# Three quarters of w_out issued behind a transpose's landing, and the second batch's k, q and v loaded a period later

## The chip, the cores and the metric

The kernel runs on one core of a Trainium2 chip. The metric is the device time of one execution in microseconds (us). The engines are PE (matrix products and transposes), DVE and ACT (element-wise work), POOL (element-wise work, and it issues DMAs) and SP (it issues DMAs). A DMA is issued from an engine's queue, in that queue's order, and lands some microseconds later.

## The reference

Thresholded attention for 8 batches of 8 heads (576 rows of 64) feeds a two-layer network over 4608 rows.

```
scores = (q @ k^T) / sqrt(64)
keep scores >= max(row) - tau, the others become -1e9        # tau = 0.02
attn = softmax(scores);   x = attn @ v                       # heads side by side: 4608 x 512
h = x @ w_in              # 512 x 2048
g = max(0.01 * h, h)
out = g @ w_out           # 2048 x 512
```

## The kernel before, in words

The work is cut into *periods*, numbered through the whole run by `n`. A period is one block of 128 rows of one batch for two pairs of heads (four heads); a batch has eight such periods, and for each two batches there are two more for the last 64 rows. Periods 0 to 7 are batch 0, period 8 is the first of batch 1. The loop at L633 issues, in an order written out by hand, the work of several stages that belong to different periods, and each engine runs its part of this list strictly in order.

For period `n` the stages are:

- **Scores** (`scores`, L302; the matmuls are at L297). Two row halves of PE run side by side. At one point the halves use the same bank of PSUM, so the last piece of the first half waits for a *signal*: an empty instruction on another engine that itself waits for the matmul before it. The list `SIGNAL` says which engine gives it in which period: POOL, except in period 2 and from period 9 on, where it is SP. An engine that gives the signal gives it in its own order, behind whatever it has queued.
- **Copies, exponentials, weights** (L338, L367, L378, L372 and L373) on DVE and ACT.
- **The turn** (`turn_w`, L387). The 128 x 2304 weights are transposed by a DMA that SP issues (L389), for every period from period 3 on; the earlier periods are transposed on PE. The turn of period `n` is issued in iteration `n + 1`. I write "turn 4" for the turn of period 4's weights.
- **pv** (`pv`, L418, matmuls at L426). The product with v of period `n` stands in iteration `n + 2` and needs turn `n`.
- **The network.** When the four pairs of a row block are ready, `layer1` (L456, matmuls L466) runs in four units and `layer2` (L473, matmuls L479) in eight; unit `r` of layer 2 reads `w_out16[:, 2r : 2r + 2]`. Each half of an iteration has two units of layer 2 and one of layer 1. The first row block's layer 2 has units 0 and 1 in iteration 4, 2 to 5 in iteration 5, and 6 and 7 in iteration 6.

Within an iteration PE's order is: scores, transposes of q and k, then the first half (layer 2, layer 1, at times a late transpose of q or k, L211, then pv) and the second half (layer 2, layer 1).

The weights w_in and w_out are loaded by POOL in four quarters each (`load_w`, L121), with a cast from fp32 to fp16; a quarter of w_out has the 512 rows that two units of layer 2 read, one pair of units for each quarter. Quarters 0 and 1 of w_out are issued in iteration 1, quarters 2 and 3 in iteration 4.

The inputs q, k and v are loaded by SP in 512 KB tiles, one for four heads. The dictionaries `loads_at`, `small_at`, `split_at_` and `pool_at` say in which iteration a load or a piece of POOL's work is put into the list; loads by SP stand behind that iteration's turn. For batch 1 the tuple `rows` gives the iterations of k (heads 0 to 3), q (heads 0 to 3), k (heads 4 to 7), q (heads 4 to 7), and `v_at` those of the two halves of v and of its last rows. The last tile of q is loaded in four parts (L86) since PE transposes part of it straight from fp32 (`late32`). POOL splits the others in an iteration before they are transposed: scaled (L160), rounded (L167), rest (L171). The second tile of k is split in iteration 6; behind that split POOL has a widening copy (L253) and two small loads (L93), and then the signal of period 7.

Of the kernel before, what the change touches and what calls it, by code (L numbers as in the profile page):

```python
# [33 lines left out]
def kernel(  # L34
# [10 lines left out]
    nc = tc.nc  # L45
# [24 lines left out]
    def load_main(b, s, which):  # L70
        if (b, s, which) in MIXED:
            return [load_part(b, s, which, t=t) for t in range(4)][0]
        t = sb.tile([128, 4, 256], FP32, tag="raw", bufs=4, name="raw")
        raws[b, s, which] = t
        return nc.sync.dma_start(
            out=t[:, :, :], in_=SRC[which][b, ds(4 * s, 4), 0:MAIN, :].rearrange("h (p t) d -> p h (t d)", t=4))
# [12 lines left out]
    def load_tails(b, which, engines=None, small=nc.sync):  # L89
        t = sb.tile([128, 2, 2, 64], FP32, tag="rawt", bufs=4, name="rawt")  # L90
        src = SRC[which][b, :, MAIN:S, :].rearrange("(u sh) p d -> u p sh d", u=2)
        for u, eng in enumerate(engines or (small, small)):
            eng.dma_start(out=t[ds(64 * u, 64), :, :, :].rearrange("p s h d -> p (s h) d"), in_=src[u])  # L93
        tails[b, which] = t

    def load_v(b, s):
        t = sb.tile([128, 4, 256], FP32, tag="vraw", bufs=2, name="vraw")
        vraws[b, s] = t
        return nc.sync.dma_start(
            out=t[:, :, :], in_=v[b, ds(4 * s, 4), 0:MAIN, :].rearrange("h (p t) d -> p h (t d)", t=4))  # L100

    def load_vtails(b, small=nc.sync):
        t = sb.tile([128, NP, 64], FP32, tag="vrawt", bufs=1, name="vrawt")
        src = v[b, :, MAIN:S, :].rearrange("(r h) p d -> h p r d", h=2)
        for h in range(2):
            small.dma_start(out=t[ds(64 * h, 64), :, :], in_=src[h])
        vtails[b] = t

    def cast_v(b, p, copy=None):
        copy = copy or nc.gpsimd.tensor_copy  # L110
        src = vraws[b, p // 2][:, ds(2 * (p % 2), 2), :].rearrange("p h (t d) -> p h t d", d=64)
        dst = v16[b % 2][:, p, :, :].rearrange("p (h t) d -> p h t d", h=2)
        return [copy(out=dst[:, h, ds(h, 4), :], in_=src[:, h, :, :]) for h in range(2)][0]  # L113

    def cast_vtails(b, copy=None):
        copy = copy or nc.gpsimd.tensor_copy
        t = vtails.pop(b)
        for h in range(2):
            copy(out=v16[b % 2][ds(64 * h, 64), :, 4 + h, :], in_=t[ds(64 * h, 64), :, :])

    def load_w(i):  # L121
        if i < 4:
            return nc.gpsimd.dma_start(out=w_in16[:, :, ts(i, 512)],
                                in_=moe_w_in[:, ts(i, 512)].rearrange("(a p) f -> p a f", p=128))
        else:
            j = i - 4
            return nc.gpsimd.dma_start(out=w_out16[:, ds(4 * j, 4), :],
                                in_=moe_w_out[ds(512 * j, 512), :].rearrange("(j p) f -> p j f", p=128))
# [62 lines left out]
    def unit32(b, which, p0, np=1, t0=0, nt=4):  # L191
        return (b, which, p0, np, t0, nt)
# [64 lines left out]
    periods, first_of = [], []  # L257
# [18 lines left out]
        cut = (a // 512 + 1) * 512  # L276
        return [(a, cut - a), (cut, a + 576 - cut)]

    SIGNAL = [nc.gpsimd, nc.gpsimd, nc.sync] + [nc.gpsimd] * 6 + [nc.sync]
    HALVES = ((0, 0), (1, 0), (0, 1))  # L280

    BEHIND = mybir.DependencyInfo(mybir.DependencyClass.Sync, mybir.DependencyReason.DATA)
# [19 lines left out]
    def scores(st, between=None):  # L302
# [12 lines left out]
        while todo[0] or todo[1]:  # L315
# [14 lines left out]
            if (h, x) == (1, b12) and i == 2:  # L330
                signal = SIGNAL[min(st.n, 9)].nop()
                tc.add_manual_dep(signal.ins, last.ins.name, BEHIND, reason="the row halves share a bank")
# [53 lines left out]

    def turn_w(st):  # L387
        st.wt = sb.tile([128, 2, 9, 128], FP16, tag="wT", bufs=4, name="wT")
        nc.sync.dma_start_transpose(  # L389
            out=st.wt[:, :, :, :].rearrange("k c n q -> k (c n) q"),  # L390
            in_=st.w[:, :, :, :].rearrange("q c n d -> q (c n d)"))

# [112 lines left out]
    loads_at, small_at, turns_at, early32, late32, split_at_, pool_at = {}, {}, {}, {}, {}, {}, {}  # L505

    def at(d, n, f):
        d.setdefault(n, []).append(f)
# [80 lines left out]
    for p in range(NP):  # L589
        at(pool_at, 1 + p // 2, lambda p=p: cast_v(0, p))  # L590
    at(pool_at, 1, lambda: cast_vtails(0))
    for i in range(4):
        at(pool_at, 1 if i < 2 else 4, lambda i=i: load_w(4 + i))

    def split_at(n, key):
        at(split_at_, n - 1, key)
        at(turns_at, n, key)
# [6 lines left out]
    for b in range(1, B):  # L604
        E = 18 * (b // 2)
        if b == 1:
            units = [(0, "k", 4), (0, "q", 5), (1, "q", 6), ("t", "k", 6), (2, "k", 7), (3, "k", 8), ("t", "q", 9)]
            late32[5], late32[7], late32[8] = [unit32(1, "k", 1)], [unit32(1, "q", 2)], [unit32(1, "q", 3)]
            rows, t_at, v_at, casts = (0, 2, 4, 5), (3, 7), (6, 7, 8), (8, 8, 9, 10, 9)
        elif b % 2 == 0:  # L610
            units = [(*u, E - 8 + i) for i, u in enumerate(in_turn)] + [("t", "k", E - 5), ("t", "q", E + 9)]
            rows, t_at, v_at = (E - 11, E - 10, E - 7, E - 6), (E - 8, E + 6), (E - 5, E - 1, E - 4)
            casts = E - 1, E, E + 1, E + 2, E
        else:
            units = [(*u, E + i + i // 4) for i, u in enumerate(in_turn)] + [("t", "k", E + 4), ("t", "q", E + 9)]
            rows, t_at, v_at = (E - 3, E - 2, E + 2, E + 3), (E + 1, E + 6), (E + 1, E + 4, E + 2)
            casts = E + 3, E + 3, E + 6, E + 7, E + 5
        for p, w_, n in units:
            split_at(n, (b, p, w_))
        for i, (s, w_) in enumerate(((0, "k"), (0, "q"), (1, "k"), (1, "q"))):  # L620
            at(loads_at, rows[i], lambda b=b, s=s, w_=w_: load_main(b, s, w_))
        for w_, n in zip("kq", t_at):
            at(small_at, n, lambda b=b, w_=w_, small=nc.sync: load_tails(b, w_, small=small))
        for s in range(2):
            at(loads_at, v_at[s], lambda b=b, s=s: load_v(b, s))
        at(small_at, v_at[2], lambda b=b, small=nc.sync: load_vtails(b, small=small))
        for p in range(NP):
            at(pool_at, casts[p], lambda b=b, p=p: cast_v(b, p))
        at(pool_at, casts[4], lambda b=b: cast_vtails(b))
# [3 lines left out]
    while n < N + PV_LAG or l1q or pending or l2q or stores:  # L633
        st = periods[n] if n < N else None
# [55 lines left out]
        for i, f in enumerate(work):  # L690
            mm = f()
# [11 lines left out]
        if here:  # L703
            o = ps.tile([128, 1024], FP16, tag="o", bufs=1, name="wp")
            if n < 3:
                turn_w_here(before, 6, 6, o[:, 0:768])
        elif before and st:
            turn_w(before)
# [91 lines left out]
```

## Time and profile before

| | |
|---|---|
| median of three runs | 482.44 us (482.31 to 482.67) |
| the profiled execution | 484.03 us, of which the span in the profile is 482.3 us |
| PE busy | 463.1 us, 96% of the span |
| DVE, ACT, POOL busy | 433.2, 420.1, 216.2 us |
| chain of waits, by engine | PE 86%, DMA 5%, DVE 4%, ACT 2% |
| DMA queues | 83.67 MB, 173 GB/s on average |
| granted clock of PE | full speed throughout |

Times in the profile count from the start of the span. The *timeline* gives start, duration, engine, line, name and count of merged instructions, and in brackets how long the engine was idle before and what released it. The *waits* view gives total us, number and longest wait for each pair of waiting and releasing lines. The *chain* is the sequence of work and waits that ended last. For a DMA, SP's and POOL's timelines show only the time that the issue took; "DMA to landing" runs from the start of the issue until the data has arrived and is signalled. One profiled execution stands for all durations.

### The profile page before, as it was taken

Reading aid. Unit: us, or ns where it says so; the run is one execution under the profiler, and the core shown is the slowest. Engines: PE = TensorE matmul, PEld = TensorE weight load, DVE = VectorE, ACT = ScalarE, POOL = GpSimd, SP = SyncE. Lnnn points to the kernel's source line nnn. Section 1 sums busy time; section 2 is a strip of 40 time slices with the busy share of each in tenths; the row PEclk is TensorE's granted clock in tenths of the full one; section 3 lists DMA queues with packets and bytes.
Section 4 is the critical chain, followed back from the end, with each engine's and each line's share of the span. In section 5 each row is a group of like instructions: output and inputs, shape, how many; then the busy total and the mean of one; then the engine's idle time right before and its main releaser. Section 6 shows DMA issues by size and latency. Waiting matters only on the chain.

```text
span 482.3 us, 25139 instructions
## 1 busy us (share of the span) xinstructions
PE 463.1 (96%) x10810; PEld 375.7 (78%) x10810; DVE 433.2 (90%) x1309; ACT 420.1 (87%) x783; POOL 216.2 (45%) x355
## 2 busy tenths in 40 slices
PE   6889889999999999999999999999999999999996
PEld 4668667888888888888888888788888778877774
DVE  3999879999999999999999999999999989999940
ACT  4899779999999999999999999899999889988862
POOL 2645547554565464454465474454466563000000
PEclk9999999999999999999999999999999999999999
DMA  9999999798999978899799988889889995655641
GB/s 176 237 217 197 164 206 201 160 196 182 205 171 202 209 161 188 155 173 211 154 190 202 212 174 201 135 183 193 185 183 193 200 165 124 124 122 123 127 91 46
DMA packets 206271, 83.67 MB, mean 173 GB/s; under 512 B 175280, under 2 KB 200880, under 8 KB 206160
## 3 DMA queue, kind: packets, MB, share of 16 engines
q1 hardware_dynamic: 199184, 74.66, 80.1%
q0 software_dynamic: 5568, 6.95, 7.8%
q8 instruction: 84, 1.38, 1.2%
q10 hardware_dynamic: 1408, 0.46, 0.4%
q14 instruction: 27, 0.22, 0.1%
HBM read 36.70 MB, written 9.44 MB: 96 GB/s over the span
## 4 chain that ended last, share of the span: by engine, by line
PE 86%; DMA 5%; DVE 4%; ACT 2%; issue 1%; SPq 1%; DVEq 0%; ACTq 0%
PE hp L466 25%; PE o L479 25%; PE sc L297 21%; PE pv L426 8%; DMA wT<-w 4%; PE tp L410 3%; PE tp L186 3%; DVE s L338 2%; DVE w L378 1%; DMA raw<-in_k_dram 1%; ACT g L469 1%; DVE qT L239 0%; SPq L86 0%; ACT e L367 0%; DVE kT L239 0%
## 5 line engine op out<-in xcount | busy, mean ns | idle before, releaser
L338 DVE TENSOR_SCALAR_CACHE_REDUCE s<-sc 128x576 f32<-128x576 f32 x288 | 205.5, 753 | 17.4 <-PE sc L297 17.4
L466 PEld LDWEIGHTS <-win 128*64 128x64 f16 x4608 | 146.5, 110 | 28.7 <-DVE xt L437 1.1
L378 DVE SCALAR_TENSOR_TENSOR w<-s,th,e 128x576 f16<-128x576 f32 x213 | 163.8, 817 | 0.2
L367 ACT ACTIVATE e<-s,mn 128x576 f16<-128x576 f32 x213 | 157.8, 778 | 0.0
L479 PE MATMUL o<-wout,g 128*64 128x512 f16 x1152 | 148.8, 379 | 0.3 <-DMA wout<-in_moe_w_out_dram 0.3
L466 PE MATMUL hp<-x,win 128*64 128x128 f16 x4096 | 136.3, 219 | 0.6 <-DVE x L445 0.3
L469 ACT ACTIVATE g<-hp 128x512 f16<-128x512 f32 x144 | 86.1, 598 | 43.7 <-PE hp L466 43.7
L297 PE MATMUL sc<-kT,qT 64*128 64x384 f16 (+7 forms) x1920 | 120.7, 284 | 3.5 <-DVE s L338 1.3
L297 PEld LDWEIGHTS <-qT 64*128 64x128 f16 (+1 forms) x1920 | 90.1, 97 | 20.3 <-issue 2.0
L160 POOL TENSOR_SCALAR scaled<-raw 128x512 f32<-128x512 f32 x53 | 32.7, 616 | 144.8 <-DVE w L378 131.8
L479 PEld LDWEIGHTS <-g 128*64 128x64 f16 x1152 | 58.7, 110 | 29.1 <-issue 0.4
L171 POOL TENSOR_TENSOR half<-scaled,half 128x512 f16<-128x512 f32 (+1 forms) x68 | 71.6, 1054 | 5.8
L373 ACT ACTIVATE w<-s,minus_tau 128x576 f16<-128x576 f32 x75 | 58.2, 776 | 2.4
L372 ACT ACTIVATE s<-s,th 128x576 f32<-128x576 f32 x75 | 57.5, 767 | 0.7 <-DVE th L356 0.7
L426 PE MATMUL pv<-wT,v 128*64 128x128 f16 (+1 forms) x1600 | 53.1, 215 | 5.2 <-DMA wT<-w 3.7
L426 PEld LDWEIGHTS <-v 128*64 128x64 f16 x1600 | 45.8, 110 | 6.9 <-issue 3.7
L167 POOL CAST half<-scaled 128x512 f16<-128x512 f32 (+1 forms) x68 | 38.3, 563 | 4.4
L445 DVE TENSOR_TENSOR x<-pv,by 128x256 f16<-128x256 f32 x64 | 27.1, 424 | 8.1 <-PE pv L426 7.0
L416 ACT COPY by<-tp 128x256 f16<-128x256 f16 x72 | 26.8, 372 | 0.0
L186 PEld LDWEIGHTS <-half 64*128 64x128 f16 x968 | 24.2, 95 | 2.5 <-issue 1.0
L113 POOL CAST v<-vraw 128x256 f16<-128x256 f32 x64 | 24.5, 417 | 0.0
L186 PE MATMUL tp<-ident,half 64*128 64x64 f16 x968 | 24.1, 190 | 0.0
(61 smaller groups left out, 332.9 us busy)
## 6 DMA issues: line engine op xcount, KB each, us to landing
vraw<-in_v_dram SPq DMA_DIRECT2D x16, 512.0 KB, 5.4
out_dram<-osb SPq DMA_DIRECT2D x31, 256.0 KB, 3.9
raw<-in_q_dram SPq DMA_DIRECT2D x13, 512.0 KB, 4.9
raw<-in_k_dram SPq DMA_DIRECT2D x13, 512.0 KB, 5.6
win<-in_moe_w_in_dram POOLq DMA_DIRECT2D x4, 512.0 KB, 10.7
wout<-in_moe_w_out_dram POOLq DMA_DIRECT2D x4, 512.0 KB, 12.5
raw<-in_q_dram SPq DMA_DIRECT2D x12, 128.0 KB, 3.8
raw<-in_k_dram SPq DMA_DIRECT2D x10, 128.0 KB, 4.3
```

The lines of the kernel that those rows point to most:

```text
L171: nc.gpsimd.tensor_tensor(out=halves[key][:, 1, 0:n, :, :], in0=scaled.pop(key)[:, 0:n, :, :], in1=halves[key][:, 0, 0:n, :, :], op=AX.sub ...
L186: nc.tensor.transpose(tps[key][r][:, x, t, :], half[rows, x, t, :, :].rearrange("p h d -> p (h d)"), ident[rows, rows])
L297: yield nc.tensor.matmul(out=o, lhsT=lhs, rhs=turned[st.b, "k"][rows, kx, pair, ds(key0, n)], start=(i == 0), stop=(i == 2), skip_group_ch ...
L338: return nc.vector.tensor_scalar(out=st.s[TILES[n]][:, :], in0=sc[:, ds(PLACE[TILES[n]], 576)], scalar1=-1.0 / UNIT, scalar2=None, op0=AX. ...
L367: nc.scalar.activation(out=st.e[t][:, :], in_=st.s[t][:, :], func=AF.Exp, bias=st.mn[:, n : n + 1], scale=-1.0)
L372: nc.scalar.activation(out=z, in_=z, func=AF.Prelu, bias=st.th[:, n : n + 1], scale=-1.0, alpha=1e20)
L373: nc.scalar.activation(out=w_of(st, t), in_=z, func=AF.Exp, bias=minus_tau[:, :], scale=1.0, accum_out=st.sum[:, c, h : h + 1])
L378: st.last = nc.vector.scalar_tensor_tensor(out=w_of(st, t), in0=st.s[t][:, :], scalar=st.th[:, n : n + 1], in1=st.e[t][:, :], op0=AX.is_le ...
L426: nc.tensor.matmul(out=st.pv[ds(64 * h, 64), c, ts(u, n)], lhsT=v16[st.b % 2][:, pair, blk, :], rhs=st.wt[:, c, blk - (blk > 4), ts(u, n)] ...
L466: nc.tensor.matmul(out=hp[ds(64 * c, 64), jj, :], lhsT=w_in16[:, i, ds(128 * (4 * u + jj) + 64 * c, 64)], rhs=g.x[:, i, :], start=(i == 0) ...
L469: nc.scalar.activation(out=g.g[:, ds(4 * u, 4), :], in_=hp[:, :, :], func=AF.Prelu, bias=0.0, scale=1.0, alpha=0.01)
L479: nc.tensor.matmul(out=g.o[ds(64 * c, 64), :], lhsT=g.g[:, j, ds(64 * c, 64)], rhs=w_out16[:, j, :], start=(j == 0), stop=(j == 15), skip_ ...
```

## The change

Four edits:

1. Quarter 0 of w_out stays in iteration 1. Quarters 1, 2 and 3 are issued by POOL at the end of iteration 4, and quarter 1 waits until turn 3 has landed; 2 and 3 follow it in POOL's order.
2. For batch 1, the second tile of k moves from iteration 4 to 5, the second tile of q from 5 to 6, and the halves of v from 6 and 7 to 7 and 8. On SP each stands behind the next turn, then: k behind turn 4, q behind turn 5, v behind turns 6 and 7.
3. The signal between the row halves of period 5 is given by SP instead of POOL.
4. `turn_w` keeps a handle of its instruction so that the wait can be attached.

The instructions on PE, DVE and ACT and their order are the same as before.

```diff
-    SIGNAL = [nc.gpsimd, nc.gpsimd, nc.sync] + [nc.gpsimd] * 6 + [nc.sync]
+    SIGNAL = [nc.gpsimd, nc.gpsimd, nc.sync, nc.gpsimd, nc.gpsimd, nc.sync] + [nc.gpsimd] * 3 + [nc.sync]
...
     def turn_w(st):
         st.wt = sb.tile([128, 2, 9, 128], FP16, tag="wT", bufs=4, name="wT")
-        nc.sync.dma_start_transpose(
+        st.turn = nc.sync.dma_start_transpose(
...
+    def load_w_out(i):
+        mm = load_w(4 + i)
+        if i == 1:
+            tc.add_manual_dep(mm.ins, periods[3].turn.ins.name, BEHIND, reason="DMA would serve w_out beside the turn")
+        return mm
+
     for i in range(4):
-        at(pool_at, 1 if i < 2 else 4, lambda i=i: load_w(4 + i))
+        at(loads_at if i else pool_at, 4 if i else 1, lambda i=i: load_w_out(i))
...
-            rows, t_at, v_at, casts = (0, 2, 4, 5), (3, 7), (6, 7, 8), (8, 8, 9, 10, 9)
+            rows, t_at, v_at, casts = (0, 2, 5, 6), (3, 7), (7, 8, 8), (8, 8, 9, 10, 9)
```

## The prediction

> **What bounds the kernel now.** The page's table of engines has PE busy for 96% of the span and its chain of waits runs through PE for 86%, so what PE waits for is what time there is to win. The windows view finds where PE idles after the start: not here,
>
> ```profile
> 80.00:85.00 5.00, 5.00 (x138) 3.90 (x126) 4.79 (x17) 4.92 (x10) 4.29 (x7) 1.00 0.74 90
> ```
>
> (PE busy 5.00 of 5.00 us), but at 50 to 55 us (3.34) and 60 to 65 us (2.97). The waits of the first 110 us name the cause (total, times, longest), and the chain of that stretch shows two long turns:
>
> ```profile
> PE pv L426 <- DMA wT<-w: 3.7, 2, 2.0
> PE o L479 <- DMA wout<-in_moe_w_out_dram: 0.3, 1, 0.3
> POOL scaled L160 <- DMA raw<-in_k_dram: 4.7, 1, 4.7
> 42.73 10.75 DMA wT<-w
> 53.56 8.93 DMA wT<-w
> ```
>
> PE's timeline (start, us, name, idle before it) places them. Layer 2 reads the second quarter of w_out at 42.37, the third at 45.66 and the fourth at 50.02; pv of periods 4 and 5 stand at 53.61 and 62.53, the scores of period 7 at 56.05, and the turn of q for pair 2 at 59.84:
>
> ```profile
> 42.37 1.03 PE L479 MATMUL o<-wout,g 128*64 128x512 f16 x8
> 45.66 1.05 PE L479 MATMUL o<-wout,g 128*64 128x512 f16 x8
> 50.02 1.05 PE L479 MATMUL o<-wout,g 128*64 128x512 f16 x8 [0.25 <-DMA wout<-in_moe_w_out_dram]
> 53.61 0.75 PE L426 MATMUL pv<-wT,v 128*64 128x128 f16 x20 [1.65 <-DMA wT<-w]
> 56.05 1.64 PE L297 MATMUL sc<-kT,qT 64*128 64x384 f16 x24
> 59.84 0.66 PE L211 MATMUL tp<-ident,raw 128*128 128x128 f32 x4
> 62.53 0.75 PE L426 MATMUL pv<-wT,v 128*64 128x128 f16 x20 [2.03 <-DMA wT<-w]
> ```
>
> From about 80 us on PE is full, so a shift left there reaches the end one for one. At stake: 1.65 + 0.25 + 2.03 = 3.93 us. The timelines of SP and POOL show what is queued:
>
> ```profile
> 34.79 4.00 SPq L389 DMA_TRANSPOSE wT<-w  x1
> 38.90 0.51 SPq L75 DMA_DIRECT2D raw<-in_k_dram  x1
> 42.73 7.16 SPq L389 DMA_TRANSPOSE wT<-w  x1
> 49.98 3.47 SPq L86 DMA_DIRECT2D raw<-in_q_dram  x4
> 53.56 3.49 SPq L389 DMA_TRANSPOSE wT<-w  x1
> 37.30 1.57 POOL L127 DMA_DIRECT2D wout<-in_moe_w_out_dram  x2
> 50.22 0.62 POOL L160 TENSOR_SCALAR scaled<-raw 128x512 f32<-128x512 f32 x1 [4.66 <-DMA raw<-in_k_dram]
> 53.24 1.32 POOL L93 DMA_DIRECT2D rawt<-in_q_dram  x2
> ```
>
> A turn holds SP while it is issued (4.00, 7.16, 3.49 us), and whatever follows waits.
>
> **Term 1: the second quarter of w_out (cost).** Before, it was issued at 23.7 and landed at 38.7, 3.7 us ahead of its reader. Now its issue on POOL waits for turn 3 to land. Turn 3 was issued at 34.79, when its weights were done, and landed 9.5 us later, beside w_out. The least that any turn of the first 120 us took is 4.6, so it lands at 39.4 at the earliest; I take that, since only the first quarter, landed at 36.0, is still ahead of it. From issue to landing the eight weight loads took 6.5 (the first of w_in) to 15.0 us; the two of w_out late in the start 8.3 and 11.9:
>
> ```profile
> DMA to landing us min/median/max: 6.5/6.5/6.5
> DMA to landing us min/median/max: 8.3/8.3/8.3
> ```
>
> (first of w_in; third quarter of w_out). I take 6.5, as here too nothing is ahead in POOL's queue. It lands at 39.5 + 6.5 = 46.0 against 42.37: PE waits s = 3.6 us. Bounds 3.0 (6.0, a little under the shortest) to 6.3 (turn at 40.4, load 8.3). Nothing covers it: the PE order is the same, and what follows needs PE.
>
> The other quarters follow 2.7 us apart (36.0 to 38.7 before) up to 3.7 (the first two of w_in): 48.7 to 49.7 and 51.4 to 53.4. With PE s later their readers come at 49.3 and 53.4, so 0, and the 0.25 at 50.02 goes; up to 0.4 if the spacing is the wide one.
>
> **Term 2: pv of period 4 (gain).** PE reaches it at 51.97 before, now at 51.97 - 0.25 + 3.6 = 55.3. Turn 4 landed at 53.47, 3.4 us behind the last load beside it (k, 50.1); 3.4 behind the fourth quarter that is 54.8 with the narrow spacing, in time, and 56.8 with the wide one, 1.5 late, which the 2.0 of term 3 would still cover. Gain 1.65. Together PE is s - 1.9 = 1.7 us late when the scores of period 7 start.
>
> **Term 3: k behind turn 4 (cost).** The load of k (pairs 2 and 3) went out at 38.90 and landed at 50.1; POOL used it at once. Behind turn 4 on SP it goes out where q's parts did, about 50. Such 512 KB loads behind a turn took 5.4 (at 72.20), 7.6 (at 64.51) and 11.2 us (this one): it lands at L = 55.4 to 61.2, taken as 56.5, the middle of the two that are not behind w_out. POOL's split, widening and two small loads run to 54.56, 4.35 us from 50.22, and only behind them stands period 7's signal between row halves, which is still POOL's. PE needs it some 1.2 us into the scores (the first row half has 2688 of its 3456 columns done, 78% of 1.5 us), at 57.2 before: then 2.6 us of slack. With 0.1 for the signal the gate is L + 4.45 - 57.2 = L - 52.75 late: 3.75 (2.65 to 8.4). That is 2.0 more than the 1.7 PE is late anyway.
>
> **Term 4: q behind turn 5 (cost, covered).** Period 5's weights end at 49.8 (ACT), now 53.4, which sets turn 5's issue; 53.56 before, so no gain there. Turn 3.5, q's four parts 3.5, last landing 2.6: 63.0, against 59.84: 3.2 late (2.7 to 5.2 with turns of 3.0 to 5.5). Under term 3's 3.75: 0.
>
> **Term 5: pv of period 5 (gain).** Turn 5 lands by 53.4 + 8.9 = 62.3; PE comes at 60.5 + 3.75 = 64.2. Gain 2.03.
>
> **The rest, at nothing.** Period 5's signal moves from POOL to SP, past turn 3, which left SP at 38.79; it is wanted at about 41.6, turn 4 behind it at 42.7. If SP were still issuing, PE would wait that long. POOL, which waits from 37.3 to 39.5 and issues until 41.8, has nothing due before its split of 41.44: 0.4 late, needed by PE at 49.02. v goes out a period later, behind turns 6 and 7: landing 72 and 81, POOL's casts wait up to 1 and 2.5 us, PE reads them from about 83 and 89. Signals from period 9 on are SP's already. Turn 8 (before 74.41, landing 81.1, read 82.85) has 512 KB more ahead of it: 0, at most 1.0.
>
> **Sum.** Net = max(s - 1.9, L - 52.75, q's 3.2) - 2.03 = max(1.7, 3.75, 3.2) - 2.03 = +1.7 us. The profiled execution took 484.03 (span 482.3 and 1.7 around it); the median of the three runs is 482.44, 1.6 less. I put the sum on the median: 484.1.
>
> **Rivals.** *The quarter is quick: faster.* At least its issue (0.8) and the 2.7 between successive landings are needed: 3.5 us, landing 43.0, s = 0.6, gate -1.3. With w_out through 2.5 us sooner turn 4's issue needs the 4.00 of turn 3, k goes out at 46.8 and lands in 5.4 to 7.6 (gate -0.6 to 1.6), turn 5 goes at 50.4 and q lands at 60.0 (gate 0.2). Net about max(-1.3, 0, 0.2) - 2.0 = -1.8: 480.6. It decides from s under 3.0 with k landed by 53.8. For: POOL's queue is empty. Against: no load of eight took under 6.5. Chance 0.13.
>
> The Trainium skill (DMA: Bandwidth & Descriptors, Anatomy of one DMA — SWDGE (gpsimd) path) gives such a load about 2.0 us plus its bytes over 436 GB/s, 3.2 us by that estimate for 512 KB, and would make s 0.3; the shortest here took 6.5.
>
> *k and q in time: no change.* If k lands by 54.5 and q within 61.6, only the quarter's wait is left: 1.7 - 2.03 = -0.3, 482.1. For: turn 4's issue may end sooner without k ahead of it. Against: w_out is ahead of it instead. Chance 0.20.
>
> *k much later.* With 8 to 11 us for k behind w_out, L = 58 to 61, net +3.2 to +6.4, 485.6 to 488.8. Chance 0.15.
>
> The forecast itself has 0.52.
>
> **Numbers.** 0.2% (about 1 us) is what a measurement of this kernel can tell from no change. Faster 0.13, same 0.20, slower 0.67. The range leaves out half of the quick case and the top of the late one: 480.8 to 487.2.
>
> **What would show it.** In the profile after: PE's wait before layer 2 near 42.4 on w_out (3.6 forecast); no wait of pv near 53 and 62; a wait in period 7's scores on POOL's signal, POOL's idle before its split growing from 4.66 to 10 or so. No wait at 42.4 makes it wrong towards faster; pv still waiting for turns makes it wrong towards slower.

## The result, and the profile after

The changed kernel takes 488.27 us (median of five, 487.89 to 490.46), the kernel before 482.31 us in the same group of runs; the ratio is 1.0149 (95% interval 1.0112 to 1.0187), slower by 1.5%. The direction was right, the size was not: +1.7 us was forecast, and 488.27 lies above the range's end of 487.2. The profiled execution has a span of 486.5 us.

The waits of the first 110 us (total, times, longest), for the lines shown of before:

```profile
PE o L479 <- DMA wout<-in_moe_w_out_dram: 5.3, 1, 5.3
POOL wout L127 <- DMA wT<-w: 4.2, 1, 4.2
```

The waits of pv on turns are gone, and one wait of layer 2 on w_out stands in their place. The chain of that stretch says how it came about: turn 3 first, then the second quarter, one behind the other.

```profile
34.83 6.43 DMA wT<-w
41.55 6.33 DMA wout<-in_moe_w_out_dram
```

PE's timeline (start, us, name, idle before it):

```profile
47.91 1.92 PE L479 MATMUL o<-wout,g 128*64 128x512 f16 x8 [5.33 <-DMA wout<-in_moe_w_out_dram]
49.57 1.97 PE L466 MATMUL hp<-x,win 128*64 128x128 f16 x32
51.47 1.00 PE L211 MATMUL tp<-ident,raw 128*128 128x128 f32 x4
...
58.69 0.72 PE L426 MATMUL pv<-wT,v 128*64 128x128 f16 x20
...
61.34 1.64 PE L297 MATMUL sc<-kT,qT 64*128 64x384 f16 x24
...
66.76 0.33 PE L211 MATMUL tp<-ident,raw 128*128 128x128 f32 x1 [0.50 <-DMA raw<-in_q_dram]
67.02 0.75 PE L426 MATMUL pv<-wT,v 128*64 128x128 f16 x20
```

The reader of the second quarter starts at 47.91 instead of 42.37. What follows it is also slow: 1.92 us for the eight matmuls of layer 2 (1.03 before), 1.97 for layer 1 (1.06), 1.00 for the transposes (0.66). The windows view shows why. Behind the stretch and its length come the busy time (and the number of instructions) of PE, of PE's weight loads, DVE, ACT and POOL; the last three columns are PE's granted clock, the DMA share and GB/s:

```profile
42.00:44.00 2.00, 0.58 (x23) 0.42 (x19) 2.00 (x6) 2.00 (x5) 1.99 (x4) 1.00 0.37 15
46.00:48.00 2.00, 0.09 (x2) 0.09 (x3) 0.00 (x0) 0.00 (x0) 1.85 (x4) 0.50 1.13 156
50.00:51.00 1.00, 1.00 (x24) 1.00 (x22) 0.00 (x0) 0.00 (x0) 0.00 (x0) 0.50 1.21 195
53.00:54.00 1.00, 1.00 (x20) 0.69 (x16) 0.73 (x2) 0.99 (x2) 0.00 (x0) 1.00 0.37 57
```

During the wait the granted clock falls to half and is back only near 52.3. The first of these lines shows a second thing: at 42 to 44 us the DMA engines move 15 GB/s, a tenth of what follows, and between 39.5 and 41.5 they served two packets. POOL's and SP's timelines (SP's first row holds turns 3 and 4, with 2.87 and 8.84 us of issue):

```profile
41.55 2.32 POOL L127 DMA_DIRECT2D wout<-in_moe_w_out_dram  x3 [4.15 <-DMA wT<-w]
58.50 0.62 POOL L160 TENSOR_SCALAR scaled<-raw 128x512 f32<-128x512 f32 x1 [10.48 <-DVE s L338]
62.07 1.33 POOL L93 DMA_DIRECT2D rawt<-in_q_dram  x2
```

```profile
34.83 16.78 SPq L389 DMA_TRANSPOSE wT<-w  x2
51.71 0.53 SPq L75 DMA_DIRECT2D raw<-in_k_dram  x1
57.14 3.18 SPq L389 DMA_TRANSPOSE wT<-w  x1
60.41 2.32 SPq L86 DMA_DIRECT2D raw<-in_q_dram  x4
```

To see where the time went, I take the start of the same ACT instruction (layer 1's activation, L469, 144 of them) from the timelines of both kernels. The changed kernel is late by 0.04 us at the first; 7.24 at the fourth (44.34 to 51.58: the wait and the slow clock); 5.29 at the seventh (neither the fourth quarter's reader nor pv of period 4 waits any longer); 5.72 at the eighth (layer 1 waits for a copy of k); 4.49 at the ninth (pv of period 5 no longer waits); 5.40 at the sixteenth (periods 10 and 11); and 4.46 at the last, since the kernel before happened to wait 1.1 us for SP's signal near 383 and 390 us in its profiled execution. I call the lateness near 110 us, less that at the first instruction, the *early shift*: 5.4 us here.

Later waits of some tenths, on SP's signals and on turns, differ from execution to execution; executions of the kernel before ranged from 479.4 to 487.1 us. So the experiments are told by two numbers: the early shift in the trace, which shows the mechanism, and the timed ratio with its interval.

### The profile page after: what moved, and what is told of

Same layout as the page of the kernel before. It is cut to its first block, busy times and chain, and to the rows that moved or that the text cites. A ratio compares the mean times of both kernels' runs of the same rounds, so it can differ in the third digit from the quotient of the medians.

```text
span 486.5 us, 25139 instructions
## 1 busy us (share of the span) xinstructions
PE 465.5 (96%) x10810; PEld 377.1 (78%) x10810; DVE 433.0 (89%) x1309; ACT 420.4 (86%) x783; POOL 218.0 (45%) x355
## 4 chain that ended last, share of the span: by engine, by line
PE 83%; DMA 6%; ACT 5%; DVE 2%; SPq 2%; issue 1%; DVEq 0%; ACTq 0%
PE hp L466 25%; PE o L479 24%; PE sc L297 20%; PE pv L426 8%; PE tp L410 3%; DMA wT<-w 3%; PE tp L186 3%; DMA wout<-in_moe_w_out_dram 1%; DVE s L338 1%; ACT e L367 1%; ACT w L373 1%; DMA raw<-in_q_dram 1%; DMA raw<-in_k_dram 1%; ACT s L372 1%; SPq L86 1%
## 5 line engine op out<-in xcount | busy, mean ns | idle before, releaser
L469 ACT ACTIVATE g<-hp 128x512 f16<-128x512 f32 x144 | 86.1, 598 | 48.3 <-PE hp L466 48.3
```

Of the source, the lines that this page charges most:

```text
L469: nc.scalar.activation(out=g.g[:, ds(4 * u, 4), :], in_=hp[:, :, :], func=AF.Prelu, bias=0.0, scale=1.0, alpha=0.01)
```

## The experiments

Each is a short edit of the kernel before or of the changed kernel. None but the one with idle matmuls changes what is computed or how much.

**w_out alone.** The changed kernel with the loads where they were:

```diff
-rows, t_at, v_at, casts = (0, 2, 5, 6), (3, 7), (7, 8, 8), (8, 8, 9, 10, 9)
+rows, t_at, v_at, casts = (0, 2, 4, 5), (3, 7), (6, 7, 8), (8, 8, 9, 10, 9)
```

> Only the w_out edit and the signal; the loads of k, q and v stay in their old periods. Theory 'quarter' (the loss is layer 2's wait for the second quarter of w_out, 5.3 us, and PE's halved clock behind it, 1.9 us; the moved loads gain or cost little): the wait stays at 5 to 6 us, the clock falls again, the waits of pv vanish, and the time is 4 to 7 us above the kernel before. Rival 'loads' (the moved loads of k, q and v cost most of the loss): 0 to 3 us above the kernel before.

PE's timeline:

```profile
47.30 1.92 PE L479 MATMUL o<-wout,g 128*64 128x512 f16 x8 [4.98 <-DMA wout<-in_moe_w_out_dram]
```

Ratio 1.0097 (1.0063 to 1.0130), +4.6 us by the medians (487.50 against 482.94); early shift 3.4. The wait, the fallen clock and the vanished waits of pv are all there without any moved load: most of the loss is the w_out edit's. (pv of period 4 does not wait here although turn 4 lands only at 56.5: PE comes later still.)

**The loads alone.** The kernel before with only the `rows` and `v_at` of the change.

> Only the loads of k, q and v a period later; w_out and the signal as before. Theory 'quarter': no wait on the second quarter, no fall of the clock; turns 4 and 5 are issued and land earlier, both waits of pv shrink, perhaps a wait of 1 to 3 us on k by way of POOL's signal in period 7: -2 to +1 us against the kernel before. Rival 'loads': +2 to +5 us.

```profile
57.19 0.50 PE L297 MATMUL sc<-kT,qT 64*128 64x256 f16 x5 [1.56 <-POOLq L331]
```

Ratio 1.0036 (1.0008 to 1.0065); early shift -0.7. Both waits of pv are gone, by the order of SP's queue alone: turn 4 is no longer behind k nor turn 5 behind q's parts. But the scores of period 7 wait for POOL's signal, behind k's split: the prediction's term 3, in the open. In periods 9 to 11 the trace then loses 1.4 us of what it had won. The timed loss of 1.6 us is more than the trace has, whose execution (482.41) was the second fastest of twelve; what the others lose later isn't shown.

**Matmuls through the wait.** The changed kernel, with matmuls whose result nothing reads ahead of the second quarter's reader:

```diff
+            if n == 5 and half == 0:
+                idle(38, spare("h"))
             for _ in range(2):
                 if l2q:
                     layer2()
```

> The changed kernel with 38 pairs of matmuls that compute nothing (on zeros, into a spare bank, some 4.1 us) on PE ahead of the second quarter's reader in period 5, so that PE does not stand idle through its wait. Theory 'quarter' with the clock lost by PE's idleness: granted clock 1.0 throughout, layer 2 and layer 1 behind the wait at 1.05 and 1.09 us instead of 1.92 and 1.97, 1.5 to 2 us less than the changed kernel. Rival (the clock falls for another reason, such as the load before, or the slower stretch is not on the path): the same time within 0.5 us.

```profile
43.04 4.34 PE L523 MATMUL spare<-blank,ident 128*64 128x256 f16 x76 [0.41 <-DVE qT L249]
47.71 1.05 PE L479 MATMUL o<-wout,g 128*64 128x512 f16 x8 [0.33 <-DMA wout<-in_moe_w_out_dram]
51.74 1.05 PE L479 MATMUL o<-wout,g 128*64 128x512 f16 x8 [0.65 <-DMA wout<-in_moe_w_out_dram]
...
56.51 1.05 PE L479 MATMUL o<-wout,g 128*64 128x512 f16 x8 [0.67 <-DMA wout<-in_moe_w_out_dram]
```

The clock stays up and the matmuls take 1.05 us, so it was PE's idleness that halved it. The time did not come back: ratio 1.0167 (1.0134 to 1.0201), early shift 5.1 against 5.4. At the fourth activation the shift is 5.36 instead of 7.24, the whole 1.9 us; but now the readers of the third and fourth quarter come too early and wait 0.65 and 0.67, and at the eighth activation the two kernels are only 0.3 us apart (65.33 and 65.67), both behind a wait of layer 1 for the copy of k (0.25 and 0.24). At the ninth they are 1.05 us apart, as the changed kernel then waits 0.5 for q, and from the seventeenth to the twenty-second 0.4. So the slow clock had stood in part in front of landings that were late anyway. Behind 110 us this execution lost some 2 us more to other waits than the changed kernel's, so its timed ratio is not the clock's worth alone. Both theories missed: the clock's cause is as the first had it, its worth nearer to the second.

**No wait on the turn.** The changed kernel without the added dependence; the three quarters are issued when POOL comes to them.

```diff
-        if i == 1:
+        if i == 9:
```

> The changed kernel without the wait on turn 3: quarters 1 to 3 of w_out are issued in period 4 as soon as POOL comes to them, some 37.3 us. Theory 'quarter': quarter 1 lands 43.6 to 45.6, PE waits 1.2 to 3.2 us instead of 5.3, short enough that the clock stays up; turn 3 lands near 44 as before, in time; 4 to 7 us less than the changed kernel, -2 to +1 against the kernel before. Rival 'loads': only the shorter wait comes back, 2 to 3 us less than the changed kernel, and a wait for k or q stands in period 7.

```profile
44.98 1.05 PE L479 MATMUL o<-wout,g 128*64 128x512 f16 x8 [2.67 <-DMA wout<-in_moe_w_out_dram]
```

The wait is half as long, the clock stays at 1.00, and the early shift is 2.1 instead of 5.4. Ratio 1.0107 (1.0070 to 1.0144): better than the changed kernel by 0.2 to 0.4%, with intervals that overlap, and less than either theory of mine wanted. The added wait protected nothing here. With the quarters issued at 37.04, turn 3 landed as soon after its issue as in the changed kernel (6.38 against 6.43 us):

```profile
DMA to landing us min/median/max: 6.4/6.4/6.4
```

In the kernel before it took 9.5 us, with the second quarter beside it until 38.6; with only that quarter back in period 1 (below) it takes 7.4. So once the second quarter is deferred, the turn needs no wait behind it.

1.2 us of PE's idleness near 52 us have no releaser in the profile. They end 1.4 us after a fetch of 16 KB on the DMA queue for instructions, which took 2.67 us here where 1.0 is usual. Of the eleven gaps of PE over 0.15 us without a releaser in the thirteen traces ten end 1.2 to 1.6 us after such a fetch and one 2.1; that PE waited for instructions is likely and not shown.

**The changed kernel once more**, for comparison.

> The changed kernel once more, beside the others of this group. 'Quarter' and 'loads' alike: +5 to +6.5 us against the kernel before.

Ratio 1.0129 (1.0095 to 1.0163), early shift 5.7, the wait 5.13 us.

**v back.** The changed kernel with `v_at` as before, `(6, 7, 8)`.

> The changed kernel with v loaded in periods 6 and 7 as before; w_out, k and q as changed. Behind the first eight periods the changed kernel lost 1.2 us more in periods 10 and 11. Theory 'v' (v in period 8 stands ahead of turn 8 on SP and holds up SP's signal of period 10): that loss is gone, 1 us less than the changed kernel; the wait on the quarter and the halved clock stay. Rival 'not v' (the loss comes with any shift of PE against SP's stores): the loss stays, same time.

In the changed kernel PE lost 1.2 us in periods 10 and 11:

```profile
84.74 0.52 PE L297 MATMUL sc<-kT,qT 64*64 64x256 f16 x10 [0.31 <-SPq L331]
...
87.46 0.69 PE L466 MATMUL hp<-x,win 128*64 128x128 f16 x18 [0.37 <-issue]
```

With v back the scores of period 10 run through and the shift stays at 4.45 from the thirteenth activation to the twentieth, where it had grown from 4.24 to 5.40. So the loss was v's. The other runs bear it out: between the thirteenth and the sixteenth activation those with v moved lose 0.9 to 1.3 us and those with v in its place nothing, but for the one with k, q and SP's signal (1.3). How v costs it is shown in part: v and q stand ahead of turn 8 on SP, whose issue took 4.63 us, and SP's signal came late behind it and the stores (0.31). The gap of 0.37 in layer 1 has no releaser; it ends 1.5 us after a fetch of instructions. The other executions divide the loss otherwise. The timed ratio, 1.0116 (1.0080 to 1.0151), can't tell a gain of 1 us, and this execution waited 2.2 us for SP's signals between 245 and 285 us instead.

**k and q, with SP's signal.** The kernel before with `rows` `(0, 2, 5, 6)` and period 7's signal given by SP.

> The kernel before with the loads of k and q a period later (5 and 6), v and w_out as before, and period 7's signal moved from POOL to SP. With the loads alone, PE waited 1.6 us for POOL's signal behind k's split. Theory 'POOL' (k's late landing costs only through the signal): the wait shrinks to under 0.6 us, and with both waits of pv gone the first 80 us are 2.5 to 3.2 us shorter than before; -2.5 to -3 us in all. Rival 'k' (the split itself comes too late for the transpose of k in period 7, or SP's signal is late behind q's four parts): 1 to 1.7 us of wait stay in period 7, -1 to -2 us.

Ratio 1.0011 (0.9982 to 1.0040): no change. The wait on the signal shrinks from 1.56 to 0.43 us, as 'POOL' had it, but the lateness comes back elsewhere: 0.57 for q, 0.55 for a signal of SP in period 9, 0.73 at the transposes of period 11. The early shift is +0.5, not -2.5. Both theories missed.

**q alone.** The kernel before with `rows` `(0, 2, 4, 6)`, run twice.

> The kernel before with only q's second tile moved, from period 5 to 6, behind turn 5 on SP; k, v, w_out and the signals as before. Theory: the wait of pv of period 4 stays (1.6 us), as turn 4 still runs behind k; turn 5 is issued near 50 instead of 53.6 and lands before 60, so pv of period 5 does not wait; no wait on k or on the signal: -2 us. Rival: turn 5 still lands late, beside q and v, and the time is that of the kernel before.

> q's second tile alone in period 6, once more: both theories 0.2 to 0.5% faster than the kernel before.

Ratio 0.9973 (0.9949 to 0.9997), then 1.0008 (0.9977 to 1.0038); early shift -2.7 and -1.7. pv of period 5 stops waiting, with nothing waiting in its stead, but what the trace gains is hardly more than the timed runs can tell. Of all kernels tried it is the only one with a ratio below 1, and only once.

**The second quarter back.** The changed kernel with quarter 1 in period 1; quarters 2 and 3 wait for turn 3.

```diff
-        if i == 1:
+        if i == 2:
-        at(loads_at if i else pool_at, 4 if i else 1, lambda i=i: load_w_out(i))
+        at(loads_at if i > 1 else pool_at, 4 if i > 1 else 1, lambda i=i: load_w_out(i))
```

> The changed kernel with the second quarter of w_out back in period 1; only the third and fourth wait for turn 3, and the loads of k, q and v and the signal stay as changed. Theory 'quarter' (a deferred quarter costs its landing, about turn 3's landing + 0.3 + 6.3, less its reader's time): the second quarter has no wait; turn 3 lands near 42 behind it, the third quarter near 48.3 against its reader at 45.7: a wait of 2 to 3 us, too short for the clock to fall, and period 8 starts 0 to 1.5 us late instead of 4.5; 3 to 5 us less than the changed kernel in all. Rival (any w_out behind turn 3 costs the same): a wait near 5 us, the clock falls, same time as the changed kernel.

```profile
50.55 1.92 PE L479 MATMUL o<-wout,g 128*64 128x512 f16 x8 [4.31 <-DMA wout<-in_moe_w_out_dram]
```

Ratio 1.0158 (1.0105 to 1.0212): no better. The wait moved to the third quarter. Turn 3, behind one more quarter, landed at 42.7, the quarter 7.5 us after its issue at 42.96, so at 50.5; its reader stood ready at 46.2: 4.3 us, where I had put 2 to 3, and long enough for the clock. The rival was nearer.

**More w_out ahead of the turn.** q alone, and the third quarter in period 1 with the first two (`1 if i < 3 else 4`).

> The kernel with q's second tile alone in period 6 (k, v and the signals as before), and the third quarter of w_out issued a step earlier instead of later: in period 1, with the first two; the fourth in period 4 without a wait. Theory (turn 4 is late because two quarters and k are served beside it): the fourth quarter and k land 2 to 3 us sooner, turn 4 lands near 50 to 51, pv of period 4 no longer waits 1.2 us, and the first 80 us are 1 to 1.5 us shorter than with q alone, -4 against the kernel before in the trace. Rival: turn 3, now behind three quarters, lands after 45 and pv of period 3 waits; no better than q alone.

```profile
53.58 1.28 PE L426 MATMUL pv<-wT,v 128*64 128x128 f16 x20 [7.67 <-DMA wT<-w]
```

Ratio 1.0157 (1.0117 to 1.0198). Turn 3 landed 18.2 us after its issue and pv of period 3 waited 7.7 us: the rival, and far past it.

## Why the prediction was wrong

**Term 1, the second quarter: right mechanism, mis-sized.** It was put at 3.6 us and measured 5.3. The load itself was right (6.33 us against 6.5); turn 3 was not. I gave it the shortest landing of any turn, 4.6 us; it took 6.43, and POOL was through its wait at 41.55, not 39.5. All but 17 of its some 2300 packets were served by 39.0, and 2.3 us passed until it counted as landed: that tail I had not allowed for. The upper bound, 6.3, held it. The other quarters followed 3.2 and 4.4 us apart instead of 2.7; this was covered only because PE was later than forecast.

**The missing term: PE's clock.** The prediction took a wait of PE as its length. The wait was long enough for the granted clock to fall to half, and the 2.6 us of work behind it took 4.5, 1.9 us more. The filler shows that 0.8 us of this was cover for landings behind it at the ninth activation, where 1.05 us was left, and that 0.4 was left at the twenty-second.

**Term 2, pv of period 4: right.** The shift goes from 7.28 to 5.29 us over period 6; 1.9 were forecast, 0.25 of it for the fourth quarter's reader. Each half of the change gains it alone: with the loads moved (0.25 to -1.73) turn 4 lands at 50.6 instead of 53.5, and with w_out deferred (7.35 to 5.37) PE comes later than the turn.

**Term 3, k by way of POOL's signal: right mechanism, the gate too long, hidden.** k landed at 58.3 (51.71 + 6.6), even later than the 56.5 taken, as turn 4 held SP until 51.6, and POOL's idle before the split grew to 10.48 us as foretold (the row names DVE; k had landed 0.15 us before the split). By the prediction's sum the gate would be 5.6 us. PE was by then 5.3 late from term 1, and its scores ran without a wait. The gate is in fact shorter: I had the signal behind the two small loads, 4.45 us after the landing. It stands behind them in POOL's list, but the traces record it before they start, at 61.88 against 62.07 in the changed kernel; with the loads alone it came 3.5 us after the landing (53.60 to 57.12), ahead of the widening copy too. So the signal did not wait for all that POOL had queued. That run shows the gate with its 1.56 us.

**Term 4, q: covered, nearly.** Its last part landed at 66.7 instead of 63.0, and PE waited 0.5 us, since the turn ahead of it was issued 3.7 us later than I had it.

**Term 5, pv of period 5: right.** No wait at 67.02.

**The rest at nothing: one item wrong.** v ahead of turn 8 was put at 0 with a bound of 1.0; it cost 1.2, and not by the turn's landing, as I argued: part of it came by SP's signal, part without a releaser. "Signals from period 9 on are SP's already" was where I should have asked what SP has ahead of them.

**The sum** was max(1.7, 3.75, 3.2) - 2.03 = +1.7. The longer wait alone would not have changed it (5.3 - 1.9 = 3.4, still under 3.75); with the clock's 1.9 the first term is 5.3 and decides (k's, with its landing and gate as measured, is some 4.7). That is the step that failed: the second quarter's wait was mis-sized, and the clock behind it was put at nothing without a reason. With the measured terms the early shift of 5.4 is 7.2 (wait and clock) - 2.0 (the fourth quarter and pv of period 4) + 0.4 (k) - 1.2 (pv of period 5, less the 0.8 that q took back) - 0.2 + 1.2 (v). The quick quarter and the case without change were both far off. The rival *k much later* has the measured time in its span (485.6 to 488.8) and k's landing at 58.3 in its bounds, but PE was late by w_out and the clock and not by k's signal: that its number fits is luck.

The rival that the Trainium skill gave a price for (DMA: Bandwidth & Descriptors, Anatomy of one DMA — SWDGE (gpsimd) path: about 2.0 us plus bytes over 436 GB/s, 3.2 us by that estimate for 512 KB) fails here: with the DMA engines idle when it was issued, the load took 6.33 us.

**What is shown.** Most of the loss comes with the deferral of w_out (w_out alone: 1.0097; the loads alone: 1.0036), by a wait that the deferral makes. How the loss splits between the wait and what follows isn't additive, as the filler and the run without the wait tell. The trade behind it is shown from both ends: w_out served beside turn 3 delays the turn (7.7 us of wait with one quarter more), and w_out served behind it delays layer 2 (5.3 us). Two lines of the changed kernel's DMA queues, between 49.0 and 49.5 us (packets, MB, share of 16 engines), show what "beside" means: w_out is on q0, turn 4 on q1.

```profile
q0 software_dynamic: 74, 0.08, 88.8%
q1 hardware_dynamic: 75, 0.02, 29.1%
```

The queues are served packet for packet, but w_out's packets are four times as big, so a turn gets a fifth of the bytes while w_out lasts: turn 4, issued at 42.8, landed 14.1 us later. The Trainium skill (DMA: Bandwidth & Descriptors, Queues, rings and completion order) says that an engine takes the queues in turn, a packet at a time; these rows agree.

## What to carry to other kernels

Before a load is put behind an event, add up the event's landing, the issue and the load's own landing, each from a row under the same traffic, and hold the sum against the reader: here 41.5 + 6.3 against 42.4. Such a chain also leaves the DMA engines idle while it waits for itself, and its cost isn't its length alone, since a PE that waits long (4.3 us and more here) comes back at half clock. Ask first whether the event needs the protection: turn 3 landed as soon without the wait, once the second quarter was out of its way. And when a load is moved past a turn on a queue that also gives signals, ask what stands behind it for another engine: k's split held up a signal on POOL (1.56 us), v and q one on SP (0.31).

## What the runs showed of the hardware

The clock: waits of PE of 2.03 and 2.67 us left it at 1.00; waits of 4.31, 4.98, 5.13, 5.33 and 7.67 us brought it to 0.50. Half-microsecond windows place the fall 1.7 to 4.8 us after PE's last matmul (near 45.4 in the changed kernel, 46.3 with w_out alone, 47.9 with the second quarter back, 50.7 with three quarters early); in all four half clock lasted 6.8 us, though PE was at work again for the last 4.0 to 5.9 us of it. The Trainium skill (TensorE: Matmul & The Clock Gate, Part 1: The HAM clock gate) has the clock halved after at least one idle window of about 3.4 us, in windows that run free of the kernel; no fall at 2.67 and one at 4.31 agree, a fall 1.7 us after the last matmul is sooner than a whole idle window.

A turn's landing has a tail: in the changed kernel all but 17 of turn 3's packets were through by 39.0 us, and its landing counted at 41.3 with the engines all but idle. A fetch of 16 KB of instructions held one DMA engine from 39.24 for 0.92 us; the turn's last two packets, of 4 bytes, were served at its end, and the landing came 1.1 us later. Turns that land 4.6 to 4.9 us after their issue have 0.5 to 0.7 us between their last data and the landing; this one had 2.0. That the fetch made the difference is likely and not tested. A turn's issue on SP stretches with the traffic ahead of it, from 2.87 us (turn 3 here) to 8.84 (turn 4), and with it everything behind on that queue.
